# A planner over engine prices writes the order of all engines, and the remaining matmuls run as 32-column pieces: an attention block with a token-mixing MLP beside it

## The chip, the cores and the metric

One core of a Trainium2 chip runs the whole program. Its engines work side by side, each through its own list of instructions in order: TensorE (PE, with its weight loads PEld), VectorE (DVE), ScalarE (ACT), GpSimd (POOL), and SyncE (SP), which here only issues DMAs. The metric is device time in microseconds (us); lower is better.

## The reference: what is computed

```python
x  = A_x                                     # 1 x 2048 x 512, bf16
xn = layernorm(x)                            # S = 2048, D = 512
q, k, v = split(xn @ wqkv)                   # 32 heads of 16
p  = softmax(q k^T / 4)                      # 2048 x 2048 for each head
A  = (p v, heads side by side) @ wo
h  = layernorm(xn)
u  = gelu(h^T @ w1 + b1)                     # per channel over the 2048 tokens, F = 1376
B  = (u @ w2 + b2)^T
out = x + A + B
```

## The kernel before

**Blocks, tiles and slots.** The queries are cut into 4 stretches of 512 (`qb`), the 32 heads into 8 groups of four, which makes NBLK = 32 blocks. A block runs over 16 key tiles of 128; for each, four score matmuls (one head each, 32 rows of the array, L802) fill two score tiles of 128x1024, so a block has 32 score tiles, numbered n over the whole program. A score tile lies in two of the eight PSUM banks. Six banks make three such slots, used in turn (n % 3; two slots in block 0), one bank gathers the PV sums of a block (`PV_BANK`) and one is for everything else (`EX_BANK`).

**Two ways to the exponential.** 26 of a block's 32 tiles go through ACT (`exp_act`, L825). Six fixed positions (`DPOS = (2, 7, 12, 17, 22, 27)`, none in block 0) go through DVE (`exp_dve`): L834 makes an integer whose bits are nearly the exponential (`dW`), L837, L841, L843 and L846 make two correction terms (`dA`, `dM`). An ACT tile costs two PV matmuls (L850, 32 columns of the array each, tiles r = 0, 1 or 2, 3); a DVE tile costs six, for the three terms W, A and M; M is multiplied with VM, a copy of V scaled by POOL (L500).

**Closing a block.** After its last PV matmul DVE copies the bank (L735, `OT32`). Four DMAs bring the row sums to `dcomp`, DVE inverts them (L747), one DMA takes them to HBM, four bring them back broadcast (`denb`), and DVE multiplies (L757, `oT`). SP issues all of these DMAs; most pass through the helper's line L301.

**Other matmuls.** All go through `EX_BANK`: Q (L463), K (L445) and V (L615) projections of later heads, MLP1 (L651, 16 matmuls for each of 11 tiles of F), MLP2 (L678, 11 for each of 16 token tiles) and the out-projection (L698, 8 for each token tile). They use the full 128x128 array with 512 columns of data, V with 128. DVE evacuates: Q twice through a mask (L476), MLP2 with x (L683) and then b2 (L686) into an fp32 residual, the out-projection with that residual (L712). DVE also makes h (L399).

**The order.** A loop over periods, one for each key tile, appends to each engine's list: two score tiles with their exponentials, then the PV matmuls that are due (two periods after the scores, four for a DVE tile), then up to two matmuls of one waiting task. The tasks (`sched_list`) have fixed start periods. Semaphores are derived afterwards from what each instruction reads and writes.

```python
LAG = 2
LAGD = 4
EXTRA_BUDGET = 2.0
...
            if period < NGRP:
                for i in range(2):
                    score_group(period, (2 * i, 2 * i + 1))
                    n = 2 * period + i
                    if is_d(n):
                        ch = exp_dve(n)
...
                        exp_act(n)
...
                if pv_i < len(pv_steps) and pv_steps[pv_i][0] <= period:
                    pv_step(pv_steps[pv_i][1])
```

Of the kernel before, what the change touches and what calls it, by code (L numbers as in the profile page):

```python
# [13 lines left out]
S = 2048  # L14
# [15 lines left out]
DEBUG_SCHED = False  # L30
# [9 lines left out]
DPOS = (2, 7, 12, 17, 22, 27)  # L40
D_FIRST_BLOCK = 1
LAG = 2
LAGD = 4
NPB = 9
NDB = 2
NQS = 3
EXTRA_BUDGET = 2.0
COOL = 1
UT_P = 10
YT_P = 10  # L50
OP_B = (118, 64, 32)
EPI_W1 = 3
EPI_W2 = 6
NW1 = 2
NW2 = 2


class Op:
    __slots__ = ("eng", "fn", "pos", "deps", "signals", "waits", "is_dma", "dma_sem",
                 "dma_val", "q", "after", "name")  # L60

    def __init__(self, eng, fn, name=""):
# [11 lines left out]
        self.name = name  # L74


class Sched:
# [11 lines left out]
    def add(self, eng, fn, reads=(), writes=(), name="", dma=False, extra_deps=(), out_dma=False):  # L89
        op = Op(eng, fn, name)  # L90
        op.is_dma = dma
        op.q = "o" if out_dma else "i"
# [15 lines left out]
        for d in extra_deps:  # L108
            if d is not None:
                deps.add(d)  # L110
        deps.discard(op)
        if eng == "pe" and not dma:
            deps = {d for d in deps if d.eng != "pe" or d.is_dma}
        op.deps = list(deps)
# [90 lines left out]
def bass_parallel_sum__softmax_full_mha__mixer_token_mlp__prompt_kernel(  # L205
# [18 lines left out]
    with ExitStack() as es:  # L224
# [6 lines left out]
        big = sb("big", [128, 2 * NT * D], BF16)  # L231
        xn_sb = big[:, 0:NT * D].rearrange("p (t d) -> p t d", d=D)
        h_sb = big[:, NT * D:2 * NT * D].rearrange("p (t d) -> p t d", d=D)
        resid = big.bitcast(F32)[:, :].rearrange("p (t d) -> p t d", d=D)

        def resid_alias_keys(st):
            ks = []
            for j in (2 * st, 2 * st + 1):
                ks.append(("xn", j) if j < NT else ("h", j - NT))
            return ks  # L240
        xnT = sb("xnT", [128, NCT, S], BF16)
        wqkv_sb = sb("wqkv_sb", [128, NCT, 3 * D], BF16)
# [886 lines left out]
```

## Time and profile before

| | us |
|---|---|
| median of 3 runs | 910.96 |
| the three runs | 911.04, 910.96, 905.46 |
| the profiled execution | 911.73 |
| its span, first to last instruction | 909.9 |

An instruction's duration in the profile runs from its start to the end of its result, and the next one on the same engine may start before that. The steady pace of an engine is therefore read from starts. A window's row gives busy times of all engines in a stretch, with the number of instructions in brackets and the granted TensorE clock as a share of 2.4 GHz.

### The profile page before, as it was taken

The numbers are of one execution on the slowest core, as the hardware profiler recorded it, in microseconds if no ns is written. First come the engines' busy times: TensorE is split into PE (matmuls) and PEld (weight loads), VectorE is DVE, ScalarE is ACT, GpSimd is POOL, SyncE is SP. The second block draws the span as 40 slices with busy tenths as digits, with TensorE's granted clock in tenths as the row PEclk, the third lists the DMA queues.
The fourth block names the chain that finished last, engine by engine and source line by source line (L and its number), as shares of the span: only waits on it lengthen the run. The fifth ranks groups of instructions, "written<-read, shape, count | busy, mean of one in ns | idle before, by whom it ended". The sixth has DMA issues, their size and how long they took to land.

```text
span 909.9 us, 14445 instructions
## 1 busy us (share of the span) xinstructions
PE 790.7 (87%) x5828; PEld 232.9 (26%) x5828; DVE 775.4 (85%) x1296; ACT 801.4 (88%) x859; POOL 35.5 (4%) x77
## 2 busy tenths in 40 slices
PE   5988888998889888988989999998998889798895
PEld 3423232322122222222222222222222222222221
DVE  6678999997778889788898889889988888888788
ACT  5987898997789888898989999898989999989895
POOL 5501110000000000000000000000000000000000
PEclk9989999997789999899999999999999999969698
DMA  6020000011111111101110110101110000000000
GB/s 162 1 53 3 30 7 8 8 31 24 30 31 27 27 30 31 25 4 36 38 39 25 29 37 20 37 25 27 39 24 5 4 7 25 13 7 9 7 8 23
DMA packets 71411, 23.08 MB, mean 25 GB/s; under 512 B 63216, under 2 KB 69360, under 8 KB 71344
## 3 DMA queue, kind: packets, MB, share of 16 engines
q1 hardware_dynamic: 68176, 20.59, 9.9%
q10 hardware_dynamic: 3168, 1.57, 0.6%
q8 instruction: 45, 0.74, 0.3%
q14 instruction: 22, 0.18, 0.1%
HBM read 19.54 MB, written 2.35 MB: 24 GB/s over the span
## 4 chain that ended last, share of the span: by engine, by line
PE 42%; DVE 29%; ACT 24%; DMA 2%; issue 2%; SPq 1%; DVEq 0%; ACTq 0%; POOL 0%
ACT pT L825 24%; PE ps L850 18%; PE ps L802 13%; DVE dW L834 11%; PE ps L651 4%; DVE dM L846 3%; PE ps L678 3%; DVE dm L843 2%; PE ps L698 2%; DVE dm L837 2%; DVE QT L476 2%; DVE dA L841 1%; DMA dcomp<-OT 1%; PE ps L615 1%; PE ps L463 1%
## 5 line engine op out<-in xcount | busy, mean ns | idle before, releaser
L825 ACT ACTIVATE pT<-ps 128x1024 bf16<-128x1024 f32 x838 | 790.6, 1045 | 82.8 <-PE ps L802 79.5
L802 PE MATMUL ps<-QT,KT 32*128 32x512 bf16 x2048 | 312.9, 403 | 91.6 <-ACT pT L825 44.2
L834 DVE TENSOR_SCALAR dW<-ps 128x1024 int16<-128x1024 f32 x186 | 227.1, 1221 | 77.8 <-PE ps L802 77.5
L850 PE MATMUL ps<-pT,V 128*32 128x512 bf16 x1676 | 250.4, 408 | 7.6 <-DVE OT L735 6.3
L802 PEld LDWEIGHTS ps<-QT,KT 32*128 32x128 bf16 x2048 | 77.5, 91 | 364.1 <-ACT pT L825 205.3
L846 DVE TENSOR_TENSOR dM<-dW,dm 128x1024 bf16<-128x1024 bf16 x186 | 128.2, 689 | 4.2
L843 DVE TENSOR_TENSOR dm<-dm 128x1024 bf16<-128x1024 bf16 x186 | 127.4, 685 | 0.0
L850 PEld LDWEIGHTS ps<-pT,V 128*32 128x32 bf16 x1676 | 62.2, 96 | 113.3 <-issue 76.8
L837 DVE TENSOR_SCALAR dm<-dW 128x1024 int16<-128x1024 int16 x186 | 80.4, 432 | 6.4
L850 PE MATMUL ps<-dM,VM 128*32 128x512 bf16 x372 | 76.5, 408 | 0.0
L850 PE MATMUL ps<-dW,V 128*32 128x512 bf16 x372 | 76.4, 407 | 0.0
L841 DVE TENSOR_SCALAR dA<-dW 128x1024 int16<-128x1024 int16 x186 | 76.3, 410 | 0.0
L850 PE MATMUL ps<-dA,V 128*32 128x512 bf16 x372 | 75.8, 404 | 0.0
L651 PE MATMUL ps<-big,w1blk 128*128 128x512 bf16 (+1 forms) x176 | 56.8, 406 | 0.0
L678 PE MATMUL ps<-gT,w1blk 128*128 128x512 bf16 (+1 forms) x176 | 55.1, 388 | 0.5 <-DVE QT L476 0.5
L698 PE MATMUL ps<-wo_pad,oT 128*128 128x512 bf16 x120 | 36.3, 384 | 0.0
L850 PEld LDWEIGHTS ps<-dW,V 128*32 128x32 bf16 x372 | 18.1, 94 | 44.5 <-issue 44.5
L850 PEld LDWEIGHTS ps<-dM,VM 128*32 128x32 bf16 x372 | 19.7, 102 | 23.8 <-issue 4.0
L476 DVE TENSOR_SCALAR QT<-ps,qmask 128x512 bf16<-128x512 f32 x30 | 21.1, 745 | 4.5 <-PE ps L463 4.3
L735 DVE COPY OT<-ps 128x512 f32<-128x512 f32 x31 | 21.3, 688 | 2.9 <-PE ps L850 2.7
L757 DVE TENSOR_TENSOR oT<-OT,denb 128x512 bf16<-128x512 f32 x31 | 21.2, 685 | 0.0
L453 DVE CAST KT<-ps 128x128 bf16<-128x128 f32 (+1 forms) x26 | 12.3, 472 | 10.3 <-PE ps L427 5.6
(73 smaller groups left out, 329.0 us busy)
## 6 DMA issues: line engine op xcount, KB each, us to landing
w1blk<-in_B_w_dram SPq DMA_DIRECT2D x10, 512.0 KB, 4.1
w1blk<-in_B_w_dram SPq DMA_DIRECT2D x16, 320.0 KB, 3.2
denb<-rden_scratch SPq DMA_DIRECT2D x124, 32.0 KB, 1.8
out_dram<-osb SPq DMA_DIRECT2D x16, 128.0 KB, 1.7
dcomp<-OT SPq DMA_DIRECT2D x124, 2.0 KB, 1.7
x_sb<-in_A_x_dram SPq DMA_DIRECT2D x3, 512.0 KB, 9.3
wqkv_sb<-in_A_wqkv_dram ACTq DMA_DIRECT2D x3, 384.0 KB, 10.8
wo_pad<-in_A_wo_dram SPq DMA_DIRECT2D x8, 64.0 KB, 2.0
```

Of the source, the lines that this page charges most:

```text
L476: sc.add("dve", lambda e, e_=e_, slot=slot: e.tensor_scalar(QT[:, slot, :], bank(bk), qmask[:, e_:e_ + 1], None, ALU.mult), reads=[("bank" ...
L651: sc.add("pe", lambda e, st=st: e.matmul(bank(EX_BANK)[0:m, :], lhsT=w1blk[:, slot, st, 0:m], rhs=h_sb[:, st, :], start=(st == 0), stop=(s ...
L678: sc.add("pe", lambda e, ft=ft, m=m: e.matmul(bank(EX_BANK), lhsT=w2blk[0:m, slot, ft, :], rhs=gT[0:m, ft, :], start=(ft == 0), stop=(ft = ...
L698: sc.add("pe", lambda e, G=G: e.matmul(bank(EX_BANK), lhsT=oT[:, par, G, 128 * sti:128 * (sti + 1)], rhs=wo_pad[:, G, :], start=(G == 0), ...
L802: sc.add("pe", lambda e, r=r, bk=bk: e.matmul(bank(bk), lhsT=KT[32 * r:32 * r + 32, T, 128 * kt:128 * (kt + 1)], rhs=QT[32 * r:32 * r + 32 ...
L825: sc.add("act", lambda e: e.activation(pT[:, buf, :], ps[:, s_ * 1024:(s_ + 1) * 1024], ACTF.Exp, scale=LN2_128), reads=[("bank", 2 * s_), ...
L834: sc.add("dve", lambda e: e.tensor_scalar(dW_i[:, buf, :], ps[:, s_ * 1024:(s_ + 1) * 1024], IBIAS, 0.0, ALU.add, ALU.max), reads=[("bank" ...
L837: sc.add("dve", lambda e: e.tensor_scalar(dm1_i[:], dW_i[:, buf, :], 0x7f, 0x3f80, ALU.bitwise_and, ALU.bitwise_or), reads=[("dW", buf)], ...
L841: sc.add("dve", lambda e: e.tensor_scalar(dA_i[:, buf, :], dW_i[:, buf, :], -128, None, ALU.bitwise_and), reads=[("dW", buf)], writes=[("d ...
L843: sc.add("dve", lambda e: e.tensor_tensor(dm1[:], dm1[:], dm1[:], ALU.mult), reads=[("dm1",)], writes=[("dm1",)], name="dm2")
L846: sc.add("dve", lambda e: e.tensor_tensor(dM[:, buf, :], dW[:, buf, :], dm1[:], ALU.mult), reads=[("dW", buf), ("dm1",)], writes=[("dM", b ...
L850: sc.add("pe", lambda e: e.matmul(bank(PV_BANK)[32 * r:32 * r + 32, :], lhsT=lhs, rhs=rhs, start=first, stop=last, tile_position=(0, 32 * r)),
```

## The change

Every instruction now carries a price, and the recorder keeps a modelled time for each engine (`_time`). The first block is still written as before. After that a loop asks each engine for the instruction that it could start earliest and appends the earliest of them all. Which score tiles go to DVE is decided as they come (at least 3 apart, not after position 28 of a block, and only when DVE has little ahead of it) instead of by fixed positions; 185 go there, 186 before. PV may take terms in the order in which they are ready, pairs of both halves together when both are.

All matmuls of `EX_BANK` but those of block 0 and the tail are cut into four pieces of 32 columns (`ext_mm`), the form that PV has. MLP2 and the out-projection of a token tile are one accumulation (`task_fin`); b2 enters as one more row of the weights, the factor 0.5 of the GELU is taken once at the end, and V's column of ones is 0.5 for that. Q is evacuated once (`Qall`) and eight DMAs bring its rows to the two masked slots. h and VM (now for all key tiles) are made by POOL. The rings are 10 (`pT`, 9 before) and 3 (DVE tiles, 2 before).

```diff
-DPOS = (2, 7, 12, 17, 22, 27)
-LAG = 2
-LAGD = 4
-NPB = 9
-NDB = 2
-EXTRA_BUDGET = 2.0
+NPB = 10
+NDB = 3
+SEM = 0.05
+PE_SWITCH = 0.11
+PE_LAT = 0.40
+EXP_I, EXP_L = 0.903, 1.03
+P1_I, P1_L = 1.13, 1.22
+DMA_L = 2.2
+D_GAP = 3
+D_LAST = 28
+D_BACKLOG = 1.2
...
+    def _time(self, op, cost, ready):
+        eng = op.eng
+        if op.is_dma:
+            op.t0 = max(self.free[eng], ready)
+            self.free[eng] = op.t0 + 0.06
+            op.t1 = op.t0 + cost[1]
+        elif eng == "pe":
+            mode, tiles, dur = cost
+            t = max(self.free["pe"], ready)
+            if mode != self.pe_mode:
+                t = max(t, self.pe_end + PE_SWITCH)
...
+            self.free["pe"] = t + 0.004
+            op.t0, op.t1 = t, t + dur + PE_LAT - 0.214
+        else:
+            op.t0 = max(self.free[eng], ready)
+            self.free[eng] = op.t0 + cost[0]
+            op.t1 = op.t0 + cost[1]
...
         def ln2_norm(t):
-            sc.add("dve", lambda e: e.tensor_scalar(h_sb[:, t, :], xn_sb[:, t, :], mv[:, t, 3:4], None, ALU.mult),
+            sc.add("pool", lambda e: e.tensor_scalar(xn_sb[:, t, :], xn_sb[:, t, :], mv[:, t, 3:4], None, ALU.mult),
...
+        def vm_scale(tiles, T):
+            t0_, n = tiles[0], len(tiles)
+            sc.add("pool", lambda e: e.tensor_scalar(
+                vm_kh[:, t0_:t0_ + n, 8 * T:8 * T + 8, :], v17_kh[:, t0_:t0_ + n, 8 * T:8 * T + 8, :], CM, None, ALU.mult),
...
+        def ext_mm(dst_rows, lhs_of, rhs, reads, start, stop, name):
+            specs = []
+            for c in range((dst_rows + 31) // 32):
+                w = min(32, dst_rows - 32 * c)
+                specs.append(dict(eng="pe", fn=lambda e, c=c, w=w: e.matmul(
+                    bank(EX_BANK)[32 * c:32 * c + w, :], lhsT=lhs_of(32 * c, 32 * c + w), rhs=rhs,
+                    start=start, stop=stop, tile_position=(0, 32 * c)),
+                    reads=reads, writes=[("bank", EX_BANK)], name=name, cost=("C", (c,), 0.214)))
+            return specs
...
+        def task_qt(qb, T):
...
+            yield "ev", [dict(eng="dve", fn=lambda e: e.tensor_scalar(Qall[:], bank(EX_BANK), QSCALE, None, ALU.mult),
...
+            for e_ in range(2):
+                slot = (8 * qb + 2 * T + e_) % 4
+                for r in range(4):
+                    a = 32 * r + 16 * e_
+                    yield "sp", [dict(dst=QT[a:a + 16, slot, :], src=Qall[a:a + 16, :], reads=[("Qall",)],
...
+        def task_fin(i):
...
+            for ft in range(NFT):
+                k = 128 if ft < NFT - 1 else FLAST + 1
+                yield "pe", ext_mm(128, lambda a, z, ft=ft, k=k: wblk[0:k, slot, ft, a:z], gT(ft)[0:k, :],
...
+            for G in range(ng):
+                yield "pe", ext_mm(128, lambda a, z, G=G: oT[:, qb % 2, G, 128 * sti + a:128 * sti + z], wo_pad[:, G, :],
+                                   [("oTc", qb % 2, G), ("wo_pad", G)], False, G == ng - 1, "op")
...
+                yield "ev", [dict(eng="dve", fn=lambda e: e.scalar_tensor_tensor(
+                    osb[:, ob, :], bank(EX_BANK), 0.5, x_sb[:, st, :], ALU.mult, ALU.add),
...
+            t_est, _, kind, what = min(cands, key=lambda z: z[0])
...
+                if n - last_d >= D_GAP and n % BN <= D_LAST and free_d and backlog <= D_BACKLOG:
+                    last_d = n
+                    buf = free_d.pop(0)
```

Three places show the new order. The first is PE's list in the stretch of MLP1 (`big` and `hx` hold h, `wblk` the weights). Before, each period has one group of four scores, its PV, and two full matmuls:

```order
L802 MATMUL ps<-QT,KT 128x512 x4
L850 MATMUL ps<-dW,V 32x512 x2
L850 MATMUL ps<-dA,V 32x512 x2
L850 MATMUL ps<-dM,VM 32x512 x2
L850 MATMUL ps<-pT,V 32x512 x4
L651 MATMUL ps<-big,w1blk 128x512 x2
L802 MATMUL ps<-QT,KT 128x512 x4
```

The same stretch in the changed kernel:

```order
L683 MATMUL ps<-hx,wblk 32x512 x16
L592 MATMUL ps<-QT,KT 128x512 x2
L654 MATMUL ps<-pT,V 32x512 x4
L683 MATMUL ps<-hx,wblk 32x512 x4
L592 MATMUL ps<-QT,KT 128x512 x2
L683 MATMUL ps<-hx,wblk 32x512 x8
L592 MATMUL ps<-QT,KT 128x512 x4
L654 MATMUL ps<-pT,V 32x512 x2
```

Scores now come mostly in pairs, each as soon as its slot is free, and pieces of the other matmuls stand between them in groups of four.

The second is DVE's list at the close of a block (the copy of the PV bank, the inversion of the row sums, the product into `oT`). Before:

```order
L735 COPY OT<-ps 128x512
L841 TENSOR_SCALAR dA<-dW 128x1024
L843 TENSOR_TENSOR dm<-dm 128x1024
L846 TENSOR_TENSOR dM<-dW,dm 128x1024
L834 TENSOR_SCALAR dW<-ps 128x1024
L837 TENSOR_SCALAR dm<-dW 128x1024
L747 RECIPROCAL rcomp<-dcomp 128x16
```

In the changed kernel, at one of its blocks:

```order
L824 COPY OT<-ps 128x512
L619 TENSOR_SCALAR dW<-ps 128x1024
L622 TENSOR_SCALAR dM<-dW 128x1024
L625 TENSOR_SCALAR dA<-dW 128x1024
L628 TENSOR_TENSOR dM<-dM 128x1024
L830 RECIPROCAL rcomp<-dcomp 128x16
```

The inversion stands where the planner took the row sums to have arrived: here four instructions after the copy, five before.

The third is SP's list around the close of a block. Before, the two halves of the chain (`dcomp`, then `rden_scratch` and `denb`) stand with loads of weights and stores of the output:

```order
L301 DMA rden_scratch<-rcomp 128x16
L301 DMA denb<-rden_scratch 16x512 x4
L301 DMA w1blk<-in_B_w_dram 128x10x128
L301 DMA w1blk<-in_B_w_dram 96x128
L714 DMA out_dram<-osb 128x512
L301 DMA dcomp<-OT 32x1x16 x4
```

In the changed kernel, in nine of the 31 closings:

```order
L348 DMA dcomp<-OT 32x1x16 x4
L348 DMA QT<-Qall 16x512 x8
L348 DMA rden_scratch<-rcomp 128x16
L348 DMA denb<-rden_scratch 16x512 x4
L348 DMA wblk<-in_B_w_dram 128x10x128
L348 DMA wblk<-in_B_w_dram 96x128
L348 DMA wblk<-in_B_b_dram 1x128
```

Eight DMAs of Q's rows stand in the queue between the two halves of the chain, and each MLP2 load has one small DMA more, for b2.

## Rows read from the trace of the kernel before

**Rows 1.** The page: span, busy time by engine, and the chain that ended last.

```profile
span 909.9 us, 14445 instructions
...
PE 790.7 (87%) x5828; PEld 232.9 (26%) x5828; DVE 775.4 (85%) x1296; ACT 801.4 (88%) x859; POOL 35.5 (4%) x77
...
PE 42%; DVE 29%; ACT 24%; DMA 2%; issue 2%; SPq 1%; DVEq 0%; ACTq 0%; POOL 0%
```

**Rows 2.** Waits: engine, line, waited for: us in total, times, longest.

```profile
PEld ps L802 <- ACT pT L825: 205.3, 450, 2.1
...
ACT pT L825 <- PE ps L802: 79.5, 150, 2.3
```

**Rows 3.** Windows, one block each: us, busy by engine, clock, DMA share, GB/s.

```profile
769.00:794.00 25.00, 20.67 (x163) 5.93 (x162) 22.44 (x36) 23.53 (x26) 0.00 (x0) 1.00 0.04 12
794.00:820.80 26.80, 24.06 (x155) 6.03 (x154) 20.84 (x34) 24.40 (x27) 0.00 (x0) 0.75 0.03 6
820.80:845.20 24.40, 20.00 (x158) 5.84 (x156) 21.84 (x35) 23.92 (x27) 0.00 (x0) 1.00 0.04 8
219.90:252.20 32.30, 27.67 (x181) 6.84 (x180) 24.75 (x39) 24.67 (x27) 0.00 (x0) 0.84 0.10 22
...
452.50:479.50 27.00, 24.04 (x178) 6.72 (x178) 24.19 (x39) 24.59 (x27) 0.00 (x0) 1.00 0.14 32
```

**Rows 4.** Windows of block 0 and after the last scores.

```profile
14.60:46.40 31.80, 27.80 (x264) 13.79 (x264) 22.28 (x68) 29.23 (x32) 14.28 (x29) 0.89 0.05 2
896.40:910.00 13.60, 5.68 (x34) 1.65 (x32) 9.45 (x17) 2.66 (x3) 0.00 (x0) 0.74 0.11 39
```

**Rows 5.** Timeline of ACT: start, us, instruction.

```profile
825.43 21.19 ACT L825 ACTIVATE pT<-ps 128x1024 bf16<-128x1024 f32 x23 [0.48 <-PE ps L802]
```

**Rows 6.** Timeline of PE and its weight loads at full clock, 500 to 502 us and at 896 us.

```profile
500.44 0.39 PE L802 MATMUL ps<-QT,KT 32*128 32x512 bf16 x4
500.77 0.39 PE L850 MATMUL ps<-pT,V 128*32 128x512 bf16 x2
501.09 0.60 PE L698 MATMUL ps<-wo_pad,oT 128*128 128x512 bf16 x2
501.63 0.71 PE L802 MATMUL ps<-QT,KT 32*128 32x512 bf16 x4
...
895.77 0.10 PEld L850 LDWEIGHTS ps<-pT,V 128*32 128x32 bf16 x4 [0.23 <-issue]
```

**Rows 7.** Groups of instructions: DVE's work that goes or moves, POOL's small operations.

```profile
L476 DVE TENSOR_SCALAR QT<-ps,qmask 128x512 bf16<-128x512 f32 x30 | 21.1, 745 | 4.5 <-PE ps L463 4.3
L683 DVE SCALAR_TENSOR_TENSOR big<-ps,x_sb 128x512 f32<-128x512 f32 x16 | 11.0, 687 | 3.6 <-PE ps L678 3.3
L686 DVE TENSOR_SCALAR big<-big,b2col 128x512 f32<-128x512 f32 x16 | 7.8, 486 | 0.6
L500 POOL TENSOR_SCALAR VM<-V 128x68 bf16<-128x68 bf16 x24 | 11.2, 487 | 121.2 <-DVE V L453 115.6 <-DVE rcomp L747 5.4
L377 POOL TENSOR_SCALAR mv<-mv 128x1 f32<-128x1 f32 x16 | 4.5, 282 | 12.1 <-DVE mv L375 12.1
```

**Rows 8.** Timeline of SP and DVE at the close of one block.

```profile
483.45 2.41 SPq L301 DMA_DIRECT2D dcomp<-OT  x4
485.10 1.22 DVE L834 TENSOR_SCALAR dW<-ps 128x1024 int16<-128x1024 f32 x1
486.35 0.43 DVE L837 TENSOR_SCALAR dm<-dW 128x1024 int16<-128x1024 int16 x1
486.99 0.25 DVE L747 RECIPROCAL rcomp<-dcomp 128x16 f32<-128x16 f32 x1 [0.21 <-DMA dcomp<-OT]
487.27 0.36 SPq L301 DMA_DIRECT2D rden_scratch<-rcomp  x1
489.56 1.71 SPq L301 DMA_DIRECT2D denb<-rden_scratch  x4
```

More of the change, by code (lines that the diff above doesn't have):

```diff
@@ L74, in __init__ @@
         self.name = name
+        self.t0 = 0.0
+        self.t1 = 0.0
 class Sched:
@@ L87, in __init__, with _deps @@
         self.dma_ops = []
[L89 to L92, printed above, removed]
+        self.free = {e: 0.0 for e in self.ENGS}
+        self.busy = {e: 0.0 for e in self.ENGS}
+        self.pe_mode = None
+        self.pe_end = 0.0
+        self.pe_tiles = {}
+    def _deps(self, eng, reads, writes, dma):
         deps = set()
@@ new lines, in pv_emit @@
+        def pv_emit(b, par, item):
+            q = pv_q[b][par]
+            q.remove(item)
+            n, term, key = item
+            first = not pv_started[b][par]
+            pv_started[b][par] = True
+            pv_left[b][par] -= 1
+            for s_ in pv_specs(item, first, pv_left[b][par] == 0):
+                add(s_)
+            if term == "P":
+                free_p.append(key[1])
+            elif not any(it[0] == n for it in q) and d_done.get(n):
+                free_d.append(key[1])
@@ L914, in bass_parallel_sum__softmax_full_mha__mixer_token_mlp__prompt_kernel @@
+        for j in range(4):
+            vm_scale(list(range(4 * j, 4 * j + 4)), 0)
+        late_consts()
+        for ft in range(NW):
+            w1_load(ft)
+        BN = 2 * NKT
+        ext_tasks = []
         for qb in range(NQB):
@@ new lines, in bass_parallel_sum__softmax_full_mha__mixer_token_mlp__prompt_kernel, with step_gen @@
+        hgen = h_work()
+        next_n = BN
+        act_q = []
+        dve_jobs = []
+        cur_ext = None
+        frees = []
+        pv_block = 0
+        pv_open = True
+        last_d = -9
+        slot_user = {}
+        log = []
+        def step_gen(g):
+            while True:
+                try:
+                    kind, what = next(g["gen"])
+                except StopIteration:
+                    g["cur"] = None
+                    return
+                if kind == "sp":
+                    for w in what:
+                        dma("sp", w["dst"], w["src"], w["reads"], w["writes"], w["name"], out_dma=w.get("out_dma", False))
+                    continue
+                if kind == "call":
+                    what()
+                    continue
+                if kind == "free":
+                    g["free"] = True
+                    continue
+                g["cur"] = (kind, what)
+                return
@@ L1077, in bass_parallel_sum__softmax_full_mha__mixer_token_mlp__prompt_kernel @@
+        assert not ext_tasks and cur_ext is None and pv_block == NBLK, (len(ext_tasks), pv_block, next_n)
+        assert sorted(resid_done) == [0, 1, 2, 3]
+        tail()
+        if DEBUG_SCHED:
+            print("modelled end", {e: round(sc.free[e], 1) for e in sc.free}, "busy", {e: round(v, 1) for e, v in sc.busy.items()},
+                  "on VectorE", len(on_d))
         sc.plan()
```

1173 lines of the change are left out of this document (567 added, 606 removed).

## The prediction

> **What bounds the kernel now.** I read the page first: busy shares and the chain that ended last. The chain changes hands all the time, 42% PE, 29% DVE, 24% ACT [rows 1]: no engine is the bound, they wait for each other. The waits say where: PE's score weights wait 205.3 us for ACT to free a slot, ACT waits 79.5 us for scores [rows 2]. PE's list is fixed, so while a score waits for a slot, the PV and MLP matmuls behind it stand still, and later they delay the next scores.
>
> Then the windows, cut at the first score of a block. A block with hardly any MLP work takes 25.0 or 24.4 us at full clock, one with 24 extra matmuls 27.0, one with such work and part of its time at 1.2 GHz (mean granted clock 0.84) 32.3 [rows 3]. Timeline of ACT: 23 exponentials in 21.19 us without a gap, 0.92 us each [rows 5]; 26 in a block make 23.9 us. That is the floor of a block as long as 26 tiles stay with ACT, and 185 against 186 tiles on DVE leave it there. The light blocks are at it; the gain to be had is what the others lie above it.
>
> **PE, by counting its list.** Timeline at full clock: four scores, 0.33 us later PV, 0.32 later a full matmul, and two of those take 0.54 until the next scores [rows 6]. So a pass of 512 columns costs 0.215 us (four 32-row or 32-column matmuls side by side make one pass) and a change of form 0.11. Before: 2170 passes, 1360 changes, 400 matmuls of 128 columns (a quarter of a pass, some 0.06): 467 + 150 + 24 = 641 us. After: 2289 passes (scores 805 for 512, since most pairs now go alone; 1476 column passes), 1612 changes, 208 short matmuls, 192 groups of four short pieces: 492 + 177 + 12 + 12 = 693 us at least. The change gives PE 52 us more to do. Cutting the others into pieces saves their change of form, but the finer order spends more changes on scores. The gain must come from waits.
>
> Per block the count gives 18 to 19 us in light blocks, 21.7 to 25.5 in blocks 5 to 12, 17 to 19 and 25 to 27, 21.8 to 23.7 in 1 to 4, and 28.8 in block 31, which gets the four last token tiles.
>
> *Pieces.* No row has groups of four pieces behind each other. Four piece loads start together and last 0.10 us [rows 6], so I take 0.215 us a group; the bound above is two passes, 0.43. For the short V pieces (48 groups in each of blocks 1 to 4) the bounds are a quarter of a pass and a whole one, 0.054 and 0.215 us, 0 to 31 us in all; I take 0.12, that is 3 us in each of the four blocks.
>
> The Trainium skill, TensorEngine Tiling (Array Packing), Restrictions, says that column tiling disables Fast Weight Load. By that the pieces load more slowly than a full matmul's weights. No row here shows it, since PV had the form already; what it would make of the sum is the second rival.
>
> **DVE.** Q's evacuations halve (10.6 us), the b2 additions go (7.8), MLP2 and out-projection share one evacuation (11.0) [rows 7], and h moves to POOL: at least 29 us off 775 [rows 1]. In a light block DVE works 22.4 of 25.0 us and isn't what ends it [rows 3], so this only helps the blocks with tasks, within the paces below.
>
> *The closing chain.* From the first `dcomp` issue to the inversion the trace has 3.5 us; 1.8 of them are three issues, so a landing takes 1.7. From the inversion it is 2.6 us to the first `denb` issue, 1.3 more to the last, and a landing: 5.6 us [rows 8]. The planner prices an SP issue at 0.06 us where the rows have 2.41 / 4 = 0.60 and 1.71 / 4 = 0.43, so its chain is short. In the block of the rows five DVE instructions stood between copy and inversion, and DVE still waited 0.21 us for the DMA [rows 8]. In the new list 15 of 31 inversions have these five or four: added up by the steps from start to start in that stretch (1.25 us for L834 [rows 8], 0.3 to 0.6 for the others) 2.5 to 3.1 us of work. Ten products stand 3.7 to 5.0 us of work behind the inversion. DVE then waits 0.2 to 1.1 us, and 0.5 to 1.8 us, in all about 10 + 11 = 21 us. Behind the waiting instruction stand the next DVE exponential, and so a score slot. DVE has 2.6 us idle in a light block [rows 3] against 0.7 us of this; I charge a quarter, 5 us. Bounds: 0, and 21 plus nine chains in which eight Q rows (8 x 0.43 = 3.4 us of SP) stand between the halves, some 2 us each, 40.
>
> *POOL.* 16 h tiles of 512 elements and 16 VM pieces of 544. POOL took 0.28 us for one element and 0.49 for 68 [rows 7]: 0.003 us an element, so 1.9 us for each, twice the planner's 0.9. Bounds: 0.49, and eight times 0.49 = 3.9 us. From 46 us on POOL has time: at 1.9 us the VM pieces of block 2 come up to 5 us late once, which is inside the allowance for blocks 1 to 4.
>
> The Trainium skill, SBUF — State Buffer, SBUF: two separate sides, says that a port pair shared by GpSimd and DVE is an exclusive lock, so one engine fully blocks. The 24 operations of L500 averaged 0.49 us beside a DVE busy 85% of the span [rows 1, 7]; no run here shows a longer block. What the rule could make of it is the fourth rival.
>
> **The sum**, in the profiled execution's time, whose first and last us stand in the rows:
> - to the end of block 0, written as before: 46.4 [rows 4];
> - blocks 1 to 4, PE some 22.8 + 3 by count, 27.0 each: 108;
> - blocks 5 to 12, count 22.3 to 25.5, ACT's floor 23.9: 25.5 each, 204;
> - 11 light blocks (13 to 16, 20 to 24, 28, 29): 24.3, as the better light row: 267;
> - 17 to 19 and 25 to 27, six at 25.2: 151;
> - block 30 24.5, block 31 (PE bound until its scores are done) 26.5;
> - from the last scores to the end 13.6 [rows 4], the same chain.
>
> That is 841. To it come DVE's 5 and the clock. Of two light blocks the one with a mean granted clock of 0.75 took 26.8 against 24.4 us [rows 3]; PE had no tasks in either, so short waits already let it fall to 1.2 GHz. Half of 26.8 us low cost 2.4, some 0.18 a us. With 11 light blocks for six I take 40 to 50 us low, 8 us. Span 854; the execution had 911.73 - 909.9 = 1.8 us around it: **856 us**. That execution lies within 0.1% of the median of the runs, 910.96, so no shift. About 1% (9 us) is what a measurement of this kernel can tell from no change.
>
> **Rivals.**
> 1. *The closing chain stalls DVE in full.* For it: the 0.60 us issues, and SP's order with Q rows. Against: DVE's idle time in every block, three DVE slots instead of two. Price 40 instead of 5: 891.
> 2. *The pieces can't be loaded in time: slower.* The place is every run of four-piece groups, 576 in all and the V pieces. At 0.43 us a group PE's count rises by 124 us, and by 0.1 x 192 = 19. Then blocks 1 to 4 take 40, 5 to 12 30.5, the six 28, block 30 24.6, block 31 39: 46 + 160 + 244 + 267 + 168 + 64 + 14 + 13 + 2 = 978. It decides from about 0.31 us a group, where the sum passes 911. For it: loads of 0.10 us are half a pass, and eight instructions must pass in 0.215 us. Against: PV's four loads go at once.
> 3. *The order doesn't keep step.* The planner's prices miss the chip by parts of a us and each engine still waits in its fixed list. Then task blocks stay at 27 to 30 us: 46 + 4 x 30 + 14 x 29 + 11 x 25 + 27 + 27 + 14 + 2 = 917, no gain. Against: its 0.214 and 0.11 are the rows' 0.215 and 0.11, its 0.903 nearly the 0.92.
> 4. *POOL is held off by DVE.* At 3.9 us an operation, the VM piece that block 2 needs at about 82 us would be ready near 119: PE stands for some 30 us once, with ACT behind it: 886. The Trainium skill's SBUF page above has the rule. Against: 0.49 us for 68 elements beside a DVE busy most of the time.
> 5. *ACT is the whole bound.* All 31 later blocks at 24.0: 46.4 + 744 + 13.6 + 1.8 = 806. Against: the counts of 25 us in blocks 8 and 9, and blocks 1 to 4.
>
> **How the numbers follow.** The forecast has 0.51 (own range 836 to 878), the chain 0.17, the pieces 0.07, the lost step 0.05, POOL 0.04, ACT's floor 0.16. Faster by over 1%, under 902: the forecast, POOL and ACT's floor, and 0.14 of the chain: 0.85. Slower by over 1%: the pieces, and 0.01 of the lost step: 0.08. Within 1%: 0.07. The range goes down to ACT's floor with a little clock, 810, and up to most of the chain's case, 900; outside stay the pieces, the lost step, and edges of the chain and of ACT's floor, together a fifth.
>
> **What would show it.** ACT's busy share should go from 88% to about 94%, with nearly the same 839 exponentials; its wait for scores from 79.5 to under 40 us; task blocks to 25 to 26 us, light ones hardly changed. DVE's inversion and product should show waits for DMAs of 10 to 20 us in all. A group of four pieces should follow another by 0.22 us: if it is 0.3 or more, the second rival holds. Long waits of PE for VM before 120 us would be the fourth. If light blocks get slower, my ACT floor or the price of changes of form is wrong; if the span is under 820, the waits that I left in were not there.

## The result, and the profile after

The changed kernel takes 879.02 us (median; four runs from 875.38 to 884.11), the kernel before, run beside it, 908.21 us (899.46 to 911.04). The ratio is 0.970, with a 95% interval of 0.961 to 0.979: faster by 3%. The forecast was 856 us with a range of 810 to 900, so the sign and the range hold, and the gain is about half of what was forecast: 29 us where 55 were expected. Ratios, and the means of the last table, count only runs within 1.5% of the fastest of the same kernel; medians and ranges are those of all runs.

The page of the changed kernel, against [rows 1]: the span, the busy shares, and the chain that ended last.

```profile
span 876.3 us, 19148 instructions
...
PE 787.1 (90%) x8124; PEld 229.7 (26%) x8124; DVE 730.6 (83%) x1227; ACT 792.9 (90%) x860; POOL 78.5 (9%) x90
...
DVE 35%; PE 34%; DMA 13%; ACT 7%; SPq 5%; POOL 5%; issue 2%; DVEq 0%
```

DVE lost 45 us of work, more than the 29 that were counted as sure. ACT's share rose from 88 to 90%, not to 94. New in the chain are DMA (13%, was 2%), SP's queue and POOL: the new list waits for things that the old one hardly waited for.

The waits (engine, line, what was waited for: us in total, times, longest), against [rows 2]:

```profile
PEld ps L592 <- ACT pT L608: 127.4, 308, 0.8
...
ACT pT L608 <- PE ps L592: 52.6, 65, 6.0
...
DVE rcomp L830 <- DMA dcomp<-OT: 24.8, 18, 3.4
...
PE ps L654 <- POOL VM L508: 12.7, 5, 5.9
...
DVE oT L838 <- DMA denb<-rden_scratch: 10.1, 11, 2.4
...
PEld ps L654 <- POOL VM L508: 8.0, 4, 3.4
```

The waits that the change was expected to cut were cut: score weights for ACT's slots from 205.3 to 127.4 us, ACT for scores from 79.5 to 52.6. Against that stand DVE's waits for the closing chain, 24.8 + 10.1 = 34.9 us, and PE's for VM, single ones of up to 5.9 us.

The windows, cut at the first scores of blocks (us, busy by engine with the number of instructions, granted clock, DMA share, GB/s), against [rows 3, 4]:

```profile
0.00:47.80 47.80, 34.90 (x332) 20.03 (x332) 31.70 (x96) 34.63 (x42) 24.94 (x56) 0.93 0.28 78
47.80:87.90 40.10, 27.89 (x430) 8.95 (x428) 27.37 (x40) 25.31 (x28) 37.54 (x26) 0.86 0.22 45
87.90:168.80 80.90, 72.91 (x1218) 26.42 (x1214) 72.48 (x114) 73.10 (x79) 15.97 (x9) 0.96 0.05 11
168.80:377.50 208.70, 198.29 (x2238) 54.66 (x2234) 181.03 (x296) 201.45 (x223) 0.00 (x0) 0.98 0.21 44
377.50:485.70 108.20, 97.75 (x648) 24.02 (x646) 85.39 (x139) 97.52 (x104) 0.00 (x0) 0.83 0.05 10
427.90:459.60 31.70, 28.08 (x162) 5.80 (x160) 22.44 (x37) 25.80 (x27) 0.00 (x0) 0.68 0.04 8
438.40:458.90 20.50, 20.50 (x104) 3.58 (x100) 14.75 (x24) 16.65 (x17) 0.00 (x0) 0.50 0.03 6
485.70:559.60 73.90, 70.50 (x776) 18.95 (x774) 64.33 (x105) 72.85 (x80) 0.00 (x0) 1.00 0.14 34
559.60:685.10 125.50, 116.09 (x824) 30.48 (x823) 108.56 (x177) 119.34 (x128) 0.00 (x0) 0.89 0.05 11
...
685.10:762.60 77.50, 72.30 (x776) 19.06 (x774) 64.34 (x105) 73.19 (x80) 0.00 (x0) 0.98 0.14 34
762.60:833.70 71.10, 65.57 (x550) 18.16 (x548) 64.92 (x106) 70.45 (x78) 0.00 (x0) 1.00 0.07 14
833.70:858.50 24.80, 23.06 (x286) 6.17 (x282) 21.64 (x35) 23.50 (x26) 0.00 (x0) 1.00 0.10 23
858.50:876.30 17.80, 7.81 (x94) 2.83 (x90) 8.85 (x15) 1.52 (x2) 0.00 (x0) 0.78 0.09 29
```

Set against the sum of the prediction, place by place (the two rows inside block 15, from 427.9 us and from 438.4, are parts of the row above them):

| place | forecast | measured | more |
|---|---|---|---|
| to the end of block 0 | 46.4 | 47.8 | 1.4 |
| block 1 | 27.0 | 40.1 | 13.1 |
| blocks 2 to 4 | 81.0 | 80.9 | 0 |
| blocks 5 to 12 | 204 | 208.7 | 4.7 |
| light blocks and block 30 | 267 + 24.5 | 304.8 | 13.3 |
| blocks 17 to 19 and 25 to 27 | 151.2 | 151.4 | 0.2 |
| block 31 to its last scores | 26.5 | 24.8 | -1.7 |
| from there to the end | 13.6 | 17.8 | 4.2 |
| DVE's 5 and the clock's 8 | 13 | in the places above | -13 |

The rows add up to the 22 us by which the span is longer than the forecast's 854. Block 1 carries 13 of them, blocks 5 to 12 and the end 9. The light blocks lie 13.3 us over their rows, but most of the 13 us for DVE and the clock was kept for them; what is of interest there is where they lost it: block 15 (31.7 us) has a stretch of 20.5 us at a granted clock of 0.50 in which PE is busy without a pause and ACT only 16.65 us.

What stood ahead of block 1's longest stop, POOL's timeline and then that of all engines (start, us, instruction, idle time before it and what ended it):

```profile
54.40 6.93 POOL L455 TENSOR_SCALAR hx<-hx,mv 128x512 bf16<-128x512 bf16 x4
61.31 1.56 POOL L508 TENSOR_SCALAR VM<-V 128x544 bf16<-128x544 bf16 x1
62.85 11.37 POOL L455 TENSOR_SCALAR hx<-hx,mv 128x512 bf16<-128x512 bf16 x7
74.20 1.56 POOL L508 TENSOR_SCALAR VM<-V 128x544 bf16<-128x544 bf16 x1
...
75.91 0.61 PE L654 MATMUL ps<-dM,VM 128*32 128x512 bf16 x2 [5.85 <-POOL VM L508]
...
77.10 1.23 DVE L619 TENSOR_SCALAR dW<-ps 128x1024 int16<-128x1024 f32 x1 [4.75 <-PE ps L592]
77.14 1.94 ACT L608 ACTIVATE pT<-ps 128x1024 bf16<-128x1024 f32 x2 [5.97 <-PE ps L592]
```

Seven h operations, 11.37 us, stand ahead of the VM piece that PE waits for. PE stands 5.85 us, and DVE and ACT stand with it.

The piece isn't block 1's own. The VM pieces of heads 0 to 7, which blocks 0 and 1 use, were done at 46.6 us; those of this timeline, from 61.31 us on, are of heads 8 to 15, for blocks 2 and 3. Block 1 waits for them because a PV matmul loads 32 columns of V or VM where a head has 17, and the changed kernel has every PV matmul depend on the next eight heads' piece too, by the key `spill`:

```python
            spill = (vk, kt, T + 1) if T < 3 else (vk, kt + 1, 0)
...
                    reads=[(vk, kt, T), key, ("Vone",), spill], writes=[("bank", PV_BANK)], name="pv" + term,
```

By the pieces that they name, all five waits of PE for VM, 12.7 us, are of this kind. The columns beyond a head's 17 don't enter the result, as the rows of `wo_pad` that meet them are zero. No run took this key away, so how much of block 1's loss it would save isn't shown.

The groups of POOL's two large operations (count, busy us, mean ns, idle before):

```profile
L508 POOL TENSOR_SCALAR VM<-V 128x544 bf16<-128x544 bf16 x16 | 26.9, 1685 | 65.2 <-DVE V L740 62.3 <-DVE V L463 2.9
...
L455 POOL TENSOR_SCALAR hx<-hx,mv 128x512 bf16<-128x512 bf16 x16 | 26.7, 1684 | 0.1
```

1.69 us each on average, where the planner reckons with 0.9.

What stood ahead of block 15's low stretch, a timeline around 436 us:

```profile
436.47 0.25 DVE L830 RECIPROCAL rcomp<-dcomp 128x16 f32<-128x16 f32 x1 [2.74 <-DMA dcomp<-OT]
...
437.86 0.39 PE L592 MATMUL ps<-QT,KT 32*128 32x512 bf16 x2 [2.17 <-DVE dW L619]
...
438.58 0.61 PE L592 MATMUL ps<-QT,KT 32*128 32x512 bf16 x4
```

DVE waits 2.74 us for the row sums, so the exponential behind the inversion is late, so PE's scores are late by 2.17 us; from 438.4 us on the granted clock is 0.50, and a set of scores lasts 0.61 instead of 0.39 us. That the wait set off the fall is the order of events here, not something that a run took apart.

### The profile page after: what moved, and what is told of

The parts are those of the page before. It is cut to its first block, busy times and chain, and to the rows that moved or that the text cites. A ratio compares the mean times of both kernels' runs of the same rounds, so it can differ in the third digit from the quotient of the medians.

```text
span 876.3 us, 19148 instructions
## 1 busy us (share of the span) xinstructions
PE 787.1 (90%) x8124; PEld 229.7 (26%) x8124; DVE 730.6 (83%) x1227; ACT 792.9 (90%) x860; POOL 78.5 (9%) x90
## 4 chain that ended last, share of the span: by engine, by line
DVE 35%; PE 34%; DMA 13%; ACT 7%; SPq 5%; POOL 5%; issue 2%; DVEq 0%
PE ps L592 13%; DVE dW L619 13%; PE ps L654 12%; PE ps L683 7%; ACT pT L608 7%; DVE dM L630 5%; SPq L348 5%; DVE dM L628 5%; DMA dcomp<-OT 4%; DVE dM L622 4%; POOL hx L455 3%; DMA wblk<-in_B_w_dram 3%; DVE dA L625 2%; DMA denb<-rden_scratch 2%; DMA rden_scratch<-rcomp 2%
## 5 line engine op out<-in xcount | busy, mean ns | idle before, releaser
L608 ACT ACTIVATE pT<-ps 128x1024 bf16<-128x1024 f32 x839 | 783.7, 1098 | 55.4 <-PE ps L592 52.6
L592 PE MATMUL ps<-QT,KT 32*128 32x512 bf16 x2048 | 348.2, 403 | 35.3 <-DVE dW L619 21.3
L654 PE MATMUL ps<-pT,V 128*32 128x512 bf16 x1678 | 274.2, 407 | 5.3 <-DVE OT L824 3.5
L592 PEld LDWEIGHTS ps<-QT,KT 32*128 32x128 bf16 x2048 | 85.2, 91 | 348.4 <-ACT pT L608 127.4
L630 DVE TENSOR_TENSOR dM<-dW,dM 128x1024 bf16<-128x1024 bf16 x185 | 127.7, 691 | 2.8
L628 DVE TENSOR_TENSOR dM<-dM 128x1024 bf16<-128x1024 bf16 x185 | 128.5, 695 | 0.0
L654 PE MATMUL ps<-dM,VM 128*32 128x512 bf16 x370 | 74.8, 408 | 16.1 <-POOL VM L508 12.7
L622 DVE TENSOR_SCALAR dM<-dW 128x1024 int16<-128x1024 int16 x185 | 80.7, 436 | 3.1
L625 DVE TENSOR_SCALAR dA<-dW 128x1024 int16<-128x1024 int16 x185 | 78.6, 425 | 0.0
L683 PE MATMUL ps<-hx,wblk 128*32 128x512 bf16 x688 | 57.8, 383 | 0.3 <-DVE u_sb L774 0.3
L683 PE MATMUL ps<-wkv_raw,wblk 128*32 128x512 bf16 x512 | 41.4, 383 | 1.8 <-DVE Qall L705 1.2
L683 PE MATMUL ps<-wo_pad,oT 128*32 128x512 bf16 x480 | 42.0, 392 | 0.0
L508 POOL TENSOR_SCALAR VM<-V 128x544 bf16<-128x544 bf16 x16 | 26.9, 1685 | 65.2 <-DVE V L740 62.3
L838 DVE TENSOR_TENSOR oT<-OT,denb 128x512 bf16<-128x512 f32 x31 | 21.3, 688 | 10.1 <-DMA denb<-rden_scratch 10.1
L830 DVE RECIPROCAL rcomp<-dcomp 128x16 f32<-128x16 f32 x31 | 7.8, 252 | 24.9 <-DMA dcomp<-OT 24.8
L455 POOL TENSOR_SCALAR hx<-hx,mv 128x512 bf16<-128x512 bf16 x16 | 26.7, 1684 | 0.1
## 6 DMA issues: line engine op xcount, KB each, us to landing
x_sb<-in_A_x_dram SPq DMA_DIRECT2D x3, 512.0 KB, 10.1
```

The lines of the kernel that those rows point to most:

```text
L455: sc.add("pool", lambda e: e.tensor_scalar(xn_sb[:, t, :], xn_sb[:, t, :], mv[:, t, 3:4], None, ALU.mult), reads=[("xn", t), ("mv", t)], w ...
L508: sc.add("pool", lambda e: e.tensor_scalar(vm_kh[:, t0_:t0_ + n, 8 * T:8 * T + 8, :], v17_kh[:, t0_:t0_ + n, 8 * T:8 * T + 8, :], CM, None ...
L592: specs.append(dict(eng="pe", fn=lambda e, r=r, bk=bk: e.matmul(bank(bk), lhsT=KT[32 * r:32 * r + 32, T, 128 * kt:128 * (kt + 1)], rhs=QT[ ...
L608: return [dict(eng="act", fn=lambda e: e.activation(pT[:, pbuf[n], :], ps[:, s_ * 1024:(s_ + 1) * 1024], ACTF.Exp, scale=LN2_128), reads=[ ...
L622: yield dict(eng="dve", fn=lambda e: e.tensor_scalar(dM_i[:, buf, :], dW_i[:, buf, :], 0x7f, 0x3f80, ALU.bitwise_and, ALU.bitwise_or), rea ...
L625: yield dict(eng="dve", fn=lambda e: e.tensor_scalar(dA_i[:, buf, :], dW_i[:, buf, :], -128, None, ALU.bitwise_and), reads=[("dW", buf)], ...
```

## Experiments

Two theories were put against each other. One: the planner's prices for POOL and SP are wrong, and the list that it writes has waits that true prices would avoid. The other: pieces, changes of form or the clock take the time, whatever the prices. All times below are medians with the range of the runs, and ratios against the kernel before on the same chip with 95% intervals. As runs differ in how long PE is held at 1.2 GHz (2 x (1 - mean granted clock) x span, there being two levels), a table after the experiments sets them on a par.

**Prices.** Three kernels with the changed kernel's code and other prices: POOL's operations as measured; SP's issue at 0.55 us and a DMA at 1.8; both.

```diff
 # VM (e1, e3)
-                cost=(0.9, 1.0))
+                cost=(1.6, 1.68))
 # h (e1, e3)
-... cost=(0.9, 1.0))
+... cost=(1.64, 1.7))
 # SP (e2, e3)
-DMA_L = 2.2
+DMA_L = 1.8
-            self.free[eng] = op.t0 + 0.06
+            self.free[eng] = op.t0 + 0.55
```

> The planner is told what POOL's h and VM operations took in the changed kernel (1.69 us, not 0.9); nothing else. Theory of the wrong prices: block 1, 40.0 us long with 11.1 us of PE standing for VM, falls to 28 to 32 us, the VM wait under 3 us, and the whole to 866 to 871 (from 879). Rival, that the clock and not a wait sets the rest: block 1 stays over 36 us or later blocks give it back, 875 to 882.

> The planner is told 0.55 us for each DMA that SP issues and 1.8 us from issue to landing (0.06 and 2.2 in the changed kernel); nothing else. Theory of the wrong prices: DVE's waits for dcomp and denb fall from 24.8 + 10.1 us to under 12 in all, and the time by 8 to 18 us, to 861 to 871, the two light blocks of 30 us with their low clock among it. Rival, that DVE's idle time covers these waits: the waits go and the time stays at 875 to 882, and light blocks still fall to 1.2 GHz.

> Both price corrections together. If both are on the path they add up: 850 to 862. If one wait only gives way to the other: no better than the better one alone. Rival: 873 to 882.

Measured: POOL alone 863.14 us (852.84 to 872.87), ratio 0.949 [0.941, 0.957]; SP alone 859.18 us (850.92 to 866.02), 0.946 [0.940, 0.952]; both 849.06 us (838.88 to 849.59), 0.934 [0.928, 0.941]. The waits of the kernel with both prices:

```profile
ACT pT L608 <- PE ps L592: 29.3, 40, 3.9
...
DVE rcomp L830 <- DMA dcomp<-OT: 8.6, 8, 3.7
...
DVE oT L838 <- DMA denb<-rden_scratch: 6.1, 8, 2.4
...
PE ps L654 <- POOL VM L508: 3.8, 2, 1.9
```

Each price takes away its own waits and not the other's: with POOL's alone PE's wait for VM falls from 12.7 to 3.8 us while DVE's for `dcomp` stays at 28.5; with SP's alone DVE's falls from 24.8 to 8.4 while PE's stays at 11.1. With both, both fall, and the time goes 30 us under that of the changed kernel. Block 1 goes from 40.1 to 33.5 us; it still has 8.6 us at the low clock and one wait of 3.7 us for `dcomp`.

**Full matmuls in the new order.** The pieces go back to full 128x128 matmuls, V's too, and the planner's estimate of their start with them; everything else stays.

```diff
-            for c in range((dst_rows + 31) // 32):
-                ...
-                    bank(EX_BANK)[32 * c:32 * c + w, :], lhsT=lhs_of(32 * c, 32 * c + w), rhs=rhs,
-                    start=start, stop=stop, tile_position=(0, 32 * c)), ... cost=("C", (c,), 0.214)))
+            specs.append(dict(eng="pe", fn=lambda e: e.matmul(
+                bank(EX_BANK)[0:dst_rows, :], lhsT=lhs_of(0, dst_rows), rhs=rhs, start=start, stop=stop),
+                reads=reads, writes=[("bank", EX_BANK)], name=name, cost=("F", (0, 1, 2, 3), 0.214)))
...
```

> The changed kernel with the matmuls of the one shared bank as full 128x128 matmuls again, as before (Q, K, V, MLP1, MLP2, out-projection), still ordered by the planner. PE's list has 836 us... by count of passes and changes of form 699 us against 693 with pieces. Theory: the order makes the gain, so within 1% of the changed kernel, 872 to 890. Rival, that pieces make it by saving changes of form: back to 895 or more.

(The count of PE's list that this text names is a slip: by the steps of the prediction it is 699 us, against 693 with pieces.) Measured: 854.64 us (851.43 to 859.03), ratio 0.944 [0.939, 0.950], faster than with pieces. The runs had some 53 us at the low clock where the changed kernel's had 115; on a par the two are 857 and 865 us, about as far apart as two orders of the same worth (865 and 872, below). So whether pieces or full matmuls are better in this order can't be told; that pieces are needed for the gain is excluded. This kernel has the old prices and nearly the old waits, 11.9 us of PE for VM and 21.0 + 9.0 of DVE for the chain.

**Pieces in the old order.** The kernel before, with its matmuls of `EX_BANK` cut into four pieces and nothing else.

```diff
-                sc.add("pe", lambda e, st=st: e.matmul(
-                    bank(EX_BANK)[0:m, :], lhsT=w1blk[:, slot, st, 0:m], rhs=h_sb[:, st, :],
+                for z in range(m // 32):
+                  sc.add("pe", lambda e, st=st, z=z: e.matmul(
+                    bank(EX_BANK)[32 * z:32 * z + 32, :], lhsT=w1blk[:, slot, st, 32 * z:32 * z + 32], rhs=h_sb[:, st, :],
...
```

> The kernel before with one part of the change alone: its other matmuls as four 32-column pieces, in the old order. PE's count falls from 640 to 605 us (1038 changes of form for 1360). If waits in the fixed order bound it: within 1% of before (907). If PE's work counts: faster by 2% or more, 890 or less. If pieces cost PE something that the count lacks, as the run with full matmuls suggests: slower, 915 or more.

Measured: 896.24 us (891.76 to 899.19), ratio 0.990 [0.984, 0.995]. By count PE's list falls from 640 to 605 us, as PV and pieces have one form and need no change between them, and 11 us of these 35 come through (907.27 in the kernel before beside it). In the fixed order the pieces are worth 1%, so the larger part of the change's gain lies in the rest of it. That rest is the order together with DVE's 45 us less work and the larger rings (10 and 3 buffers for 9 and 2); no run takes these apart, so that the order makes most of the gain is likely, by the waits that it cut and by how much other orders of the same code move the time, but not shown.

**A key for each Q row.** Both prices as above; and the eight DMAs that bring Q's rows no longer count as writing one and the same thing, by which each waited for the landing of the one before.

```diff
-                                      writes=[("QT", slot)], name="q_row")]
+                                      writes=[("QT", slot, r)], name="q_row")]
...
```

> Both price corrections, and each of the eight DMAs of Q's rows has a name of its own for what it writes, so that it no longer waits for the one before to land (12.9 us of SP for eight). If these chains still hold DVE up: 840 to 846 and DVE's waits for dcomp and denb under 8 us. If Q's rows lay off the path: 846 to 852, as with the prices alone (849).

In the changed kernel SP's queue had this wait:

```profile
SPq L348 <- DMA QT<-Qall: 121.6, 90, 3.0
```

With keys of their own it is gone from the list of SP's waits. The time is 852.21 us (844.07 to 856.95), ratio 0.938 [0.932, 0.944], that of both prices alone: in that order nobody waited for these rows.

**All of it, with full matmuls.** Both prices, the keys and the full matmuls.

> All corrections of the run before, and full 128x128 matmuls for the others. Theory that pieces cost time by themselves: 20 us under the same kernel with pieces, 820 to 830. Theory that the full-matmul run was fast only by less time at 1.2 GHz in its light blocks (56 us against 109), by the chance of its order: within 1% of the same kernel with pieces, 840 to 855.

Measured: 841.88 us (836.67 to 868.24), ratio 0.926 [0.920, 0.932]. Its waits:

```profile
ACT pT L608 <- PE ps L592: 19.4, 28, 2.8
...
DVE rcomp L825 <- DMA dcomp<-OT: 5.0, 4, 3.0
...
DVE oT L833 <- DMA denb<-rden_scratch: 4.3, 4, 2.0
...
PE ps L654 <- POOL VM L508: 4.1, 2, 2.2
```

**How far apart are two orders of the same worth?** One price that matters little, an exponential's, at 0.908 or 0.898 for 0.903 us, in the changed kernel, and at 0.908 in the version with everything. Each gives another list throughout.

```diff
-EXP_I, EXP_L = 0.903, 1.03
+EXP_I, EXP_L = 0.908, 1.03
```

> The changed kernel with one price moved by half a hundredth (exponential 0.908 us, not 0.903), which is nearer the trace and should be worth nothing: a measure of how far two orders of equal worth lie apart. If the orders' chance is small: 874 to 884. If it is as large as the gains of the price runs: anywhere from 850 to 890, and single runs of changed prices then show little.

> The changed kernel with nothing but the exponential's price at 0.898 for 0.903 us. It gives a third order of the same worth beside 879.0 and 891.3. Scatter of the order alone: 868 to 893. If it comes under 862, the gains of single prices (863.1 and 859.2) can't be told from scatter at all, and only the versions with both prices can.

> The fastest version so far with nothing changed but the planner's price of an exponential, 0.908 for 0.903 us; both stand below the 0.92 of the trace. If the gains of the prices are a matter of the prices, its time lies within 12 us of 841.9, between 830 and 856, with VM waits of PE under 5 us and DVE's wait for the row sums under 12 us. If they were luck of one order, it lies at 860 to 890, like the changed kernel and its own copy with that price (879 and 891).

Measured: the changed kernel at 0.908 takes 891.3 us (883.03 to 899.58), ratio 0.982 [0.975, 0.989]. At 0.898 its five runs go from 862.94 us, at a mean granted clock of 0.963, to 899.95, at 0.896, with a median of 887.72; only the first counts, so there is no ratio. The version with everything takes 845.86 us at 0.908 (841.13 to 853.41), ratio 0.935 [0.929, 0.940]. So three orders with the old prices lie at 863 to 889 us by the runs that count, and four with both true prices at 839 to 850 (the two with full matmuls at 839 and 847), with PE's wait for VM at 3.2 us and DVE's for `dcomp` at 6.4 in the last: the gain of both prices isn't the luck of one list. A single price's 16 to 20 us does not stand by its time, as the third old order comes down to 863; what stands is that its waits went.

**Filling the light blocks.** The changed kernel with 288 groups of four pieces more in blocks 13 to 16, 20 to 24 and 28 to 30. They write sums to the spare bank that nobody reads.

```diff
+        def task_fill():
+            for _ in range(6):
+                yield "pe", ext_mm(128, lambda a, z: wq_sb[:, 0, a:z], xnT[:, 0, 0:512],
+                                   [("wq", 0)] + [("xnT", t) for t in range(4)], True, True, "fill")
+        for b in (13, 14, 15, 16, 20, 21, 22, 23, 24, 28, 29, 30):
+            for j in range(4):
+                ext_tasks.append((BN * b + 8 * j, BN * b + 8 * j + 16, "fill", task_fill(), None))
```

> The changed kernel with 288 more groups of four pieces in the light blocks 13 to 16, 20 to 24 and 28 to 30; their sums go to the spare bank and are read by nobody, so the output is the same. By count PE's list grows from 693 to 740 us. Theory A: the stretches of some 20 us at 1.2 GHz in light blocks (two of them, blocks 15 and 21, 31.7 and 30.3 us for 24.3) come of PE having too little to do there, and cost some 14 us in all; with work for PE they go, the light blocks take 24 to 25.5 us each, the low clock in the light blocks falls from 65 to under 20 us, and the time goes to 865 to 875 in spite of 47 us more work for PE. Theory B: the low clock only follows a late DVE or DMA and is no matter of what PE has to do: then stretches like these stay, the filled blocks get longer by up to 4 us each, and the time is 885 to 915. Two orders that differ in nothing that matters lay 12 us apart, so only a gain or a loss beyond that tells by the time alone; the clock by block tells without it.

Measured: 859.72 us (857.8 to 866.37), ratio 0.951 [0.946, 0.956]. More work for PE, and 19 us less. Its windows, block 1, the filled blocks 13 to 16 with block 15 of them, blocks 17 to 19, and the filled blocks 20 to 24 and 28 to 30:

```profile
46.50:86.60 40.10, 27.79 (x430) 8.87 (x427) 27.41 (x40) 25.22 (x27) 37.48 (x26) 0.86 0.21 45
376.80:472.20 95.40, 92.15 (x1032) 25.51 (x1028) 85.28 (x139) 94.87 (x105) 0.00 (x0) 1.00 0.05 12
423.50:448.00 24.50, 23.28 (x264) 6.67 (x260) 20.29 (x33) 24.21 (x28) 0.00 (x0) 1.00 0.04 10
472.20:550.80 78.60, 74.39 (x790) 19.10 (x786) 64.20 (x104) 72.27 (x79) 0.00 (x0) 0.93 0.14 33
550.80:672.00 121.20, 116.30 (x1312) 32.26 (x1308) 106.45 (x173) 119.21 (x131) 0.00 (x0) 1.00 0.05 11
...
747.10:818.80 71.70, 70.38 (x772) 18.93 (x768) 61.21 (x101) 70.82 (x78) 0.00 (x0) 1.00 0.06 14
```

Block 1 is what it was, to 0.1 us. The light blocks and block 30 stay at full clock and take 95.4 + 121.2 + 71.7 = 288.3 us instead of 304.8. Blocks 17 to 19 are longer, 78.6 for 73.9: there DVE waited 3.25 us for `dcomp` until 534.1 us, and a stretch of 10 us at the low clock followed from 535.9. So the low clock follows a late chain outside the light blocks too. In the filled blocks no single wait of DVE for the chain was over 1.63 us, so the runs do not part what the filling did by PE's work from what it did by moving these waits.

The Trainium skill, TensorE: Matmul & The Clock Gate, Part 1, says that the clock of the array is set by how busy it has been shortly before. The windows agree: 0.83 and 0.89 in the light blocks without the filling, 1.00 with it. The stretch in block 15 does not fit as plainly: PE shows 20.50 of 20.50 us busy there, and the clock stayed at 0.50.

**Filling the fastest version.**

> The fastest version so far (both prices, a key for each Q row, full matmuls; 841.9 us, span 834.6 with 49 us at the low clock, of which 7 in light blocks) with the same filling work, as 288 full matmuls that nobody reads; by count PE's list is 746 us for some 700. Theory A: little low clock is left to win in the light blocks, so the filling only costs its room: 840 to 855, low clock in light blocks under 7. Theory B: 850 to 880, as the filled blocks get longer by 1 to 3 us each.

Measured: 837.66 us (834.72 to 851.05), ratio 0.925 [0.919, 0.931]: the same as without. There was little left to win, 7 us at the low clock in its light blocks, and the filling cost nothing that shows.

**On a par.** Among runs of one kernel the time rises with the low clock: 75 runs of 13 kernels give 0.27 us for each us at 1.2 GHz (standard error 0.02). The last column brings the mean of the runs that count to 60 us of it with that slope (the changed kernel at 0.898 has one such run and isn't among the 75). The slope is a fit, and the low clock itself follows waits, so the column shows what goes with the low clock and not what it alone costs.

| kernel | mean us | us at 1.2 GHz | at 60 us |
|---|---|---|---|
| before | 905.2 | 82 | 899 |
| before, pieces alone | 896.4 | 93 | 887 |
| changed | 879.4 | 115 | 865 |
| changed, exponential 0.908 | 889.2 | 123 | 872 |
| changed, exponential 0.898, one run | 862.9 | 64 | 862 |
| changed, filled | 861.5 | 52 | 864 |
| changed, full matmuls | 855.5 | 53 | 857 |
| POOL's price | 859.0 | 65 | 858 |
| SP's price | 856.3 | 69 | 854 |
| both prices | 845.6 | 70 | 843 |
| both, keys | 849.6 | 82 | 844 |
| both, keys, full | 838.6 | 53 | 841 |
| the same, exponential 0.908 | 846.8 | 84 | 841 |
| the same, filled | 837.5 | 36 | 844 |

All of the 18 us that the filling brings go with the low clock: on a par 865 and 864. The gain of both prices does not: 865 to 843. On a par three old orders with pieces lie at 862 to 872 and the one with full matmuls at 857, all five kernels with both true prices at 841 to 844; one price alone, 858 and 854, isn't clear of the old orders. The change itself is worth some 34 us on a par (899 to 865) and pays 9 of them back by 33 us more at the low clock.

## Why the prediction was right in its sign and half wrong in its size

*PE's steps held.* Eight groups of four pieces, from the timeline at full clock:

```profile
858.84 1.91 PE L683 MATMUL ps<-wkv_raw,wblk 128*32 128x512 bf16 x32
```

The last lasts 0.39 us, so the seven before it follow at 1.52 / 7 = 0.217 us: the value taken, not the bound of 0.43. The second rival is false. Blocks 2 to 4, 17 to 19, 25 to 27 came within 0.2 us of their terms and blocks 5 to 12 within 5.

*What failed first: "the VM pieces of block 2 come up to 5 us late once, which is inside the allowance for blocks 1 to 4".* The duration was well estimated (1.9 us, measured 1.69). The step "from 46 us on POOL has time" was not: POOL works without a gap from 46.5 to 85.7 us, the h operations among it. And the pieces of block 2 are late not once but four times, 12.5 us in all, and already for block 1, whose matmuls wait for them by `spill`; the prediction took them to be needed only when block 2 begins. PE, DVE and ACT stand, and the allowance of 27.0 us a block met 40.1. True prices bring block 1 to 33.5 us; the other half of the miss stays there, at the low clock, in the first closing chain and in 3.8 us of waits for VM, and wasn't taken apart.

*Second: "I charge a quarter, 5 us" of the closing chain.* The waits were 34.9 us against 21 estimated. SP's price took 16.7 us of them away, and its kernel lies 11 us lower on a par: two thirds instead of a quarter, but as one old order may lie 10 us from another, the share isn't fixed by it. Right behind the wait stand the exponential of a score slot and the scores, as the rows at 436 us show; how much of such a wait a light block can take, no run measured.

*Third: the clock, "40 to 50 us low, 8 us".* In the profiled execution the light blocks had 65 us at 1.2 GHz, and the slope is 0.27, not 0.18: 17 us. Filled, they took 288.3 us against the 291.5 of the sum without the clock's term, so the term of 24.3 us a block was right and the clock was mis-sized. The waits of the second point feed this one. Yet the light blocks came out within a us of their 291.5 and the 13 kept for chain and clock: by the slope the clock's term was 9 us too small, the row was 3 too long, and the chain's 5 make up most of the rest. That this adds up is luck. The sign that slower light blocks would mean a wrong floor of ACT or a wrong price of changes of form misled: filled, they keep the floor.

*Fourth, small: "the same chain" after the last scores.* Two of the closing steps of the tail, from its timeline:

```profile
866.54 0.94 DVE L860 RECIPROCAL denb<-denb 128x128 f32<-128x128 f32 x1
...
868.90 0.94 DVE L860 RECIPROCAL denb<-denb 128x128 f32<-128x128 f32 x1
```

And before:

```profile
903.30 0.94 DVE L771 RECIPROCAL denb<-denb 128x128 f32<-128x128 f32 x1
...
905.08 0.94 DVE L771 RECIPROCAL denb<-denb 128x128 f32<-128x128 f32 x1
```

One step takes 2.36 us where the kernel before took 1.78: a token tile's addition into `osb`, which waits 0.5 to 0.7 us for PE, now stands ahead of the next inversion, where before it stood one inversion later. From the first inversion to the last it is 7.3 us for 4.8, some 2.5 of the 4.2. The other 1.7 lie ahead of the first inversion, where PE has the last token tile's pieces left to do after the last scores, and DVE waits 4.3 us for it. The prediction took the chain over without looking at its order.

*Q's rows* were priced at 8 x 0.43 = 3.4 us of SP; they take 11.5 to 15.0, each waiting for the one before. The term was wrong by three to four times and, with both prices true, cost nothing, as the kernel with keys of their own shows; in the changed kernel's own order no run tried it.

*The rivals.* The first, a closing chain that stalls DVE, was right in its place and nearly in its waits (35 of 40 us). The third, "the planner's prices miss the chip", named what the price runs confirm, but bound it to the prices of PE and ACT, which were right, and to no gain at all. The fourth had POOL as the culprit through a port; POOL's operations lasted 1.56 to 2.54 us beside a DVE busy 68% of block 1 and 90% of blocks 2 to 4, so none lasted a us longer than the shortest: not the port, but the planner's 0.9, and the key that asks for block 2's pieces in block 1. The Trainium skill, SBUF — State Buffer, SBUF: two separate sides, has an exclusive lock on the port that the two engines share; the trace allows for that 1 us at most and shows no longer hold. The fifth, 806, was right for the light blocks alone: in the version with everything they and block 30 take (96.2 + 119.9 + 71.5) / 12 = 24.0 us, the rival's own figure, while head, block 1 (33.5 us) and tail stay above it.

## What to carry to other kernels

A schedule written from a price list is as good as its worst price: read each engine's price from starts in the trace, the DMA issue and the idle engine's operations too, and look for the waits that the planner believes not to exist. Ask of each wait that is left whether it is for something that the waiting instruction uses. Two lists of equal worth lie 1% or so apart at the same time spent at the low clock, and up to 3% as they come, so judge a change of order by the waits that go with it, and by more than one list. Where PE has slack, compare runs at the same time spent at the low clock before giving a difference to anything else.

## What was not expected of the hardware

Two stretches at 1.2 GHz of 20.5 and 27.3 us (from 438.4 and 592.0 us in the changed kernel's trace), in blocks where PE has little to do; the other low stretches of that trace were under 7 us. The first began 0.5 us behind a PE wait of 2.17 us, the second 2.5 us behind one of 0.99. Yet from 100 us on seven other PE waits, of 0.93 to 1.99 us, had full clock for the 4 us behind them, and three short low stretches in light blocks, from 380, 407 and 462 us, had no PE wait over 0.9 us shortly ahead, so the wait alone doesn't tell. In the first stretch PE is busy without a pause (20.50 of 20.50 us) and ACT only for 16.65 us. How much of its time a program spends at the low clock differs from run to run: the kernel before had spans from 895.7 us at a mean granted clock of 0.969 to 911.6 us at 0.939. And work that nobody needs, put where PE has room, can make a kernel faster: 879 to 860 us.
